# Gated linear attention and a multiplicative FFN on one core: pairs from running products instead of levels, in list-scheduled order

## Chip, core and metric

The kernel runs on one NeuronCore of one Trainium2 chip. The metric is the device time of one execution in microseconds (us), the median of several runs.

## What is computed

For each of 4 batches and 8 heads a state of 48 x 48 numbers runs over 768 tokens; every row d of it is multiplied by its own gate before the token's product is added. The result of all heads, 3072 tokens x 384, goes through the FFN.

```python
f = 1.0 / (1.0 + np.exp(-f_logit))
for t in range(S):
    state = f[:, :, t, :, None] * state + np.einsum('bhd,bhe->bhde', k[:, :, t], v[:, :, t])
    y[:, :, t] = np.einsum('bhd,bhde->bhe', q[:, :, t], state)
a = x @ w1
b = x @ w2
h = a * b @ w3
return (h @ w_out).astype(np.float32)
```

Here x is y with the heads side by side, w1 and w2 are 384 x 1024, w3 is 1024 x 1024 and w_out 1024 x 384. q, k, v and f_logit are float32; the four weights arrive as float64 and are turned to float32 on the chip.

## The kernel before, in words

The tokens are cut into 24 chunks of 128, six to a batch. The heads go in four pairs, the even head of a pair on partitions 0 to 47, the odd one on 64 to 111, so a tile of a chunk is 112 partitions x 512 columns (4 pairs x 128 tokens). Three chunks make an FFN block of 384 tokens; there are eight blocks.

- **Products of gates** (`prep_items`, lines 106 to 132): for a chunk, VectorE and ScalarE build seven levels. At level l the blocks of 2^l tokens hold q and k with the products of the gates inside the block; half of a new tile is multiplied by VectorE (line 125), the other half copied by ScalarE (line 129), once for q and once for k.
- **Attention** (`attend_items`): every pair of tokens of a chunk is taken at the level of the smallest block that holds both. `leaf` (line 171) makes products of 32 x 32 for six levels, and VectorE masks and adds them up (lines 178, 184); GpSimd copies the result into the pair matrix (line 192). `off` (lines 201, 209) adds the two coarse levels, `turn` (226) transposes k, `value` multiplies the pair matrix with v (263) and q with the state before the chunk (270), `advance` (240 to 251) renews the state, `join` (288) transposes the result into xt.
- **FFN** (`ffn_items`): for each of eight column groups, xt times w1 and xt times w2 (line 306), three products of 128 x 128 x 384 each; ScalarE copies the first (312), VectorE multiplies the second into it (315). `down` (323) multiplies with wc = w3 w_out.
- **Weights** (`weight_items`, `fetch`): 36 pieces of float64, first w_out (8), then w3 (16, two to a `fold` of eight products into wc, line 380), then w1 and w2 (12). A piece goes through VectorE (352, 353, 354), GpSimd (355), ScalarE (356, 357), VectorE (358) and GpSimd (359).

The order is written out by hand: for chunk u, the items of its attention, of the products of chunk u + 1 and a share of the waiting weights or FFN work carry a number between 0 and 1 and are emitted in that order. Each engine runs its instructions strictly in the order of emission. SP issues all DMAs.

A float32 matmul stands in the trace as two MATMUL instructions, each with its LDWEIGHTS (PEld).

## Time and profile before

| | us |
|---|---|
| median of three runs | 863.71 |
| lowest and highest run | 860.79, 870.68 |
| span of the profiled execution, the only time that its page gives | 863.2 |

| engine | busy, us | share of the span | instructions |
|---|---|---|---|
| TensorE (PE) | 701.1 | 81% | 12824 |
| VectorE (DVE) | 449.4 | 52% | 972 |
| ScalarE (ACT) | 275.7 | 32% | 757 |
| GpSimd (POOL) | 120.3 | 14% | 182 |

The span runs from the first to the last instruction of one execution. A busy share is an average over stages that differ: the stretch in which the weights are converted (to about 220 us), the long middle, and the last block. [...]

### The profile page before, as it was taken

How to read it: one execution, taken by the hardware profiler on the slowest of the kernel's cores; microseconds unless marked ns; L12 is line 12 of the kernel's file. 1: busy time of each engine (PE TensorE's matmuls, PEld its weight loads, DVE VectorE, ACT ScalarE, POOL GpSimd, SP SyncE). 2: the span in 40 equal slices, each digit the busy share in tenths (PEclk: the TensorE clock that was granted, in tenths of full speed). 3: DMA queues.
4: the chain of work that ended last, by engine and by line, in shares of the span. 5: the costliest groups of instructions: out<-in, count | busy, mean ns of one | idle time of the engine just before them, and what ended most of it. 6: DMA issues, size and time to landing. Idle time of an engine off the chain costs nothing.

```text
span 863.2 us, 28797 instructions
## 1 busy us (share of the span) xinstructions
PE 701.1 (81%) x12824; PEld 466.2 (54%) x12824; DVE 449.4 (52%) x972; ACT 275.7 (32%) x757; POOL 120.3 (14%) x182
## 2 busy tenths in 40 slices
PE   3236477642789988999999888989999998988998
PEld 2223343331456655666566556665666656665654
DVE  6866455489946255525652555355526652563010
ACT  3432222134524333233323333333334432431110
POOL 3432223154300000000000000000000000000000
PEclk9996686755899998999999889999999999998999
DMA  4421422144101021102110111011101111000000
GB/s 145 142 97 34 126 74 97 35 137 132 52 26 39 25 58 39 30 20 58 40 30 22 56 40 30 20 58 40 31 25 53 40 30 47 21 2 3 28 0 27
DMA packets 21580, 43.37 MB, mean 50 GB/s; under 512 B 3664, under 2 KB 9936, under 8 KB 21456
## 3 DMA queue, kind: packets, MB, share of 16 engines
q1 hardware_dynamic: 21456, 41.53, 15.5%
q8 instruction: 100, 1.64, 0.8%
q14 instruction: 24, 0.20, 0.1%
HBM read 36.80 MB, written 4.72 MB: 48 GB/s over the span
## 4 chain that ended last, share of the span: by engine, by line
PE 76%; issue 8%; DVE 7%; POOL 5%; ACT 2%; DMA 1%; SPq 0%; POOLq 0%; DVEq 0%; ACTq 0%
PE f L306 32%; PE f L323 15%; PE par L171 10%; PE f L380 7%; PE par L263 4%; DVE snap L125 3%; PE par L270 2%; POOL exponent L355 2%; ACT exponent L356 2%; PE par L209 2%; POOL w3s L359 1%; PE misc L240 1%; DVE exponent L358 1%; PE par L201 1%; PE misc L226 1%
## 5 line engine op out<-in xcount | busy, mean ns | idle before, releaser
L306 PE MATMUL f<-xt,w1s 128*128 128x384 f32 x384 | 150.1, 530 | 9.6 <-ACT xt L289 7.1
L306 PE MATMUL f<-xt,w2s 128*128 128x384 f32 x384 | 152.5, 537 | 2.4 <-DVE ab L315 2.4
L125 DVE TENSOR_TENSOR snap<-snap,tprod 112x256 f32<-112x256 f32 x288 | 127.6, 484 | 38.5 <-ACT snap L129 33.0
L178 DVE TENSOR_TENSOR sc<-par,mask 128x384 f32<-128x384 f32 x96 | 53.0, 552 | 164.2 <-PE par L171 164.2
L129 ACT COPY snap<-snap 112x256 f32<-112x256 f32 x312 | 110.8, 413 | 76.8 <-DVE snap L106 74.1
L323 PE MATMUL f<-wc,ab 128*128 128x384 f32 x384 | 128.2, 488 | 0.0
L171 PE MATMUL par<-snap 48*32 48x32 f32 x6144 | 84.4, 208 | 47.5 <-issue 44.4
L192 POOL COPY amt<-ad 32x256 f32<-32x256 f32 x96 | 45.9, 479 | 540.0 <-DVE ad L184 535.9
L380 PE MATMUL f<-ab,w3s 128*128 128x384 f32 x128 | 64.1, 674 | 57.5 <-POOL w3s L359 57.5
L306 PEld LDWEIGHTS f<-xt,w1s 128*128 128x128 f32 x384 | 74.0, 203 | 53.6 <-issue 11.2
L171 PEld LDWEIGHTS par<-snap 48*32 48x32 f32 x6144 | 74.3, 110 | 51.2 <-issue 47.8
L306 PEld LDWEIGHTS f<-xt,w2s 128*128 128x128 f32 x384 | 74.0, 203 | 47.4 <-issue 8.6
L323 PEld LDWEIGHTS f<-wc,ab 128*128 128x128 f32 x384 | 71.8, 190 | 47.6
L184 DVE TENSOR_REDUCE ad<-sc 128x64 f32<-128x384 f32 x96 | 78.1, 814 | 4.6
L380 PEld LDWEIGHTS f<-ab,w3s 128*128 128x128 f32 x128 | 33.6, 271 | 84.4 <-POOL w3s L359 60.1
L312 ACT COPY a<-f 128x384 f32<-128x384 f32 x64 | 30.6, 479 | 139.9 <-PE f L306 139.9
L315 DVE TENSOR_TENSOR ab<-f,a 128x384 f32<-128x384 f32 x64 | 35.4, 553 | 65.7 <-PE f L306 65.5
L356 ACT ACTIVATE exponent<-exponent 128x512 uint32<-128x512 uint32 (+1 forms) x36 | 21.8, 606 | 130.5 <-POOL exponent L355 130.5
L263 PE MATMUL par<-vt,amt 128*128 128x48 f32 x384 | 49.1, 283 | 17.1 <-ACT amt L219 16.9
L263 PEld LDWEIGHTS par<-vt,amt 128*128 128x128 f32 x384 | 49.9, 203 | 23.9 <-issue 17.5
L328 ACT COPY o<-f 128x384 f32<-128x384 f32 x24 | 11.5, 479 | 100.6 <-PE f L323 96.0
L171 PEld LDWEIGHTS par<-q,k 48*32 48x32 f32 x1536 | 22.5, 110 | 35.1 <-issue 28.7
(53 smaller groups left out, 651.7 us busy)
## 6 DMA issues: line engine op xcount, KB each, us to landing
raw<-in_w_dram SPq DMA_DIRECT2D x28, 512.0 KB, 3.5
f<-in_f_logit_dram SPq DMA_DIRECT2D x48, 96.0 KB, 2.6
q<-in_q_dram SPq DMA_DIRECT2D x48, 96.0 KB, 2.8
k<-in_k_dram SPq DMA_DIRECT2D x48, 96.0 KB, 2.2
vt<-in_v_dram SPq DMA_DIRECT2D x24, 192.0 KB, 3.0
out_dram<-o SPq DMA_DIRECT2D x24, 192.0 KB, 1.9
raw<-in_w_out_dram SPq DMA_DIRECT2D x8, 384.0 KB, 4.1
mask<-in_leaf_mask_dram SPq DMA_DIRECT2D x1, 96.0 KB, 2.3
```

What stands on the lines that cost most here:

```text
L125: nc.vector.tensor_tensor(dst[:, :, grow], src[:, :, grow], tt[:, :, 1 - grow : 2 - grow].to_broadcast([R, nb, m]), ALU.mult,)
L129: nc.scalar.copy(dst[:, :, 1 - grow], src[:, :, 1 - grow])
L171: nc.tensor.matmul(pp[par][a : a + 32, o : o + 32], lhsT=kk[rows(par), cols], rhs=qq[rows(par), cols], start=True, stop=True,)
L178: nc.vector.tensor_tensor(sc.rearrange("p h l i -> p h (l i)"), pp[par][:, 0 : 2 * NLEAF * 32].rearrange("p (h n) -> p h n", h=2), mask.re ...
L184: nc.vector.tensor_reduce(out=st["ad"][:, par, 2 * half : 2 * half + 2], in_=sc.rearrange("p h l i -> p h i l"), axis=AX.X, op=ALU.add,)
L192: nc.gpsimd.tensor_copy(amt[a : a + 32, :, :, a : a + 32], st["ad"][a : a + 32])
L263: nc.tensor.matmul(po(hp, par), lhsT=amt[:, par, hp], rhs=st["v"][:, h * D : h * D + D], start=(hp == 0), stop=first, skip_group_check=True,)
L306: nc.tensor.matmul(pu, lhsT=ws[:, kc, jc * P : jc * P + P], rhs=xts[n][:, kc], start=(kc == 0), stop=(kc == KM - 1),)
L315: nc.vector.tensor_tensor(st["ab"][jc], pu, st["a"], ALU.mult)
L323: nc.tensor.matmul(po, lhsT=st["ab"][jc][:, s * P : s * P + P], rhs=wc[:, jc], start=(jc == 0), stop=(jc == KF - 1),)
L356: nc.scalar.activation(s, s, AF.Copy, bias=-896.0 * 2.0**23, scale=2.0**23)
L380: nc.tensor.matmul(pw, lhsT=st["w"][:, kc * P : kc * P + P], rhs=wo[kc], start=(kc == 0), stop=(kc == KF - 1),)
```

## The change

- **One product per head and chunk.** For a chunk, two scans on VectorE run along the tokens: `forward` gives the product P of the gates from the chunk's second token on, `backward` the products of the gates after a token, divided by P at the chunk's end (`ends`). Q = q P and K = k times the backward product; K and Q are multiplied once per head (`pairs`, 128 x 128), VectorE masks the result with a triangle (`mask`), and the value product, now transposed, uses it as the moving operand. The lines 106 to 209 of before, their copies on ScalarE and GpSimd, and the transpose of the result are gone; ten DMAs per block from SBUF to SBUF put the result into xt. The state is kept in a block form for a pair of heads (`blocks`, on GpSimd), so the state's part of the value product is four matmuls a chunk, not eight.
- **A range test.** `judge` tests that no product at a chunk's end is below 2^-40 and that all results are finite, and writes a flag; every engine loads it after its last instruction (line 136) and, where it is set, runs `general`, the scheme of before without the conversion of weights, and without the interleaving of prep, attention and FFN.
- **Weights.** w1 and w2 come first, then w_out, then w3. The last multiplication of a piece is one VectorE instruction (line 521), which takes over the ScalarE scaling (357) and the GpSimd multiplication (359). Four buffers for raw words where there were three, 21 buffers for the products a b where there were 12, three PSUM buffers for the FFN where there were two.
- **Order.** `Plan.order` takes all work as tasks with an engine, a cost, dependences and a priority, and places at each step the task that can start first. The numbers of cost are the author's.

```diff
+NAB = 21
+FLOOR = 2.0**-60
+RANGE = 2.0**-40
...
+        while left:
+            best = None
+            for t in left:
+                if any(d["end"] is None for d in t["deps"]):
+                    continue
+                at = max(
+                    [free.get(t["eng"], 0.0)]
+                    + [d["end"] + (d["lag"] if d["eng"] != t["eng"] else 0.0) for d in t["deps"]]
+                )
+                if t["takes"]:
+                    n, taken = self.slots[t["takes"]]
+                    if len(taken) >= n:
+                        enders = freed[id(taken[-n])]
+                        if any(e["end"] is None for e in enders):
+                            continue
+                        at = max([at] + [e["end"] + e["lag"] for e in enders])
+                key = (at, t["prio"], t["no"])
+                if best is None or key < best[0]:
+                    best = (key, t)
+            (at, _, _), t = best
+            t["at"], t["end"] = at, at + t["cost"]
+            free[t["eng"]] = t["end"]
+            if t["takes"]:
+                self.slots[t["takes"]][1].append(t)
+            left.remove(t)
+            done.append(t)
+        return sorted(done, key=lambda t: (t["at"], t["no"]))
...
+        ranged(tc, q, k, f_logit, v, w1, w2, w3, w_out, out, ident, w1s, w2s, wc, left)
+        outside = nc.values_load(left[0:1, 0:1], min_val=0, max_val=1)
+        with tc.If(outside > 0, preferred_fallthrough_block=False):
+            general(tc, q, k, f_logit, v, leaf_mask, out, ident, w1s, w2s, wc)
...
+        t["lf"] = plan.add("SP", 1.2, load(fs[u % 2], f_logit), past(u, 2, "g"), n0 - 30, lag=2.2)
...
+        def gates():
+            g, f = gate[u % 2], heads(fs[u % 2])
+            nc.scalar.activation(heads(g[:, 0:NQ])[:, :, 1:C], f[:, :, 1:C], AF.Sigmoid)
+            nc.scalar.activation(lead[u % 4], f[:, :, 0], AF.Sigmoid)
+        t["g"] = plan.add("ACT", 0.85, gates, [t["lf"]] + past(u, 2, "r") + past(u, 5, "d"), n0)
...
+        def forward():
+            s["P"] = one.tile([R, NQ], F32, name="fwd")
+            nc.vector.tensor_tensor_scan(
+                s["P"], gate[u % 2][:, 0:NQ], first, 0.0, ALU.mult, ALU.add
+            )
+        t["p"] = plan.add("DVE", 1.1, forward, [t["g"]] + past(u, 1, "q", "i"), n0)
+        def ends():
+            last = heads(s["P"])[:, :, C - 1]
+            end = heads(back)[:, :, C - 1]
+            nc.vector.tensor_scalar(end, last, FLOOR, None, ALU.max)
+            nc.vector.reciprocal(end, end)
+            nc.vector.tensor_tensor(least, least, last, ALU.min)
+            if not closes:
+                s["G"] = work3.tile([R, HP], F32, name="G")
+                nc.vector.tensor_copy(s["G"], last)
...
+        def scale_q():
+            s["Q"] = work3.tile([R, NQ], F32, name="Q")
+            nc.vector.tensor_tensor(s["Q"], qs[u % 3], s["P"], ALU.mult)
...
+        def backward():
+            s["R"] = one.tile([R, NQ], F32, name="bwd")
+            nc.vector.tensor_tensor_scan(
+                s["R"][:, ::-1], gate[u % 2][:, NQ:0:-1], back[:, ::-1], 0.0, ALU.mult, ALU.add
+            )
...
+        def pairs():
+            s["pa"] = [ps.tile([P, NQ], F32, name=f"pa{par}") for par in range(2)]
+            for hp in range(HP):
+                cols = slice(hp * C, hp * C + C)
+                for par in range(2):
+                    nc.tensor.matmul(
+                        s["pa"][par][:, cols], lhsT=s["K"][rows(par), cols], rhs=s["Q"][rows(par), cols],
+                        start=True, stop=True,
+                    )
+        t["a"] = plan.add("PE", 1.2, pairs, [t["q"], t["k"]] + past(u, 1, "m0", "m1"), n0 - 1000)
...
+                    s["A"][:, par], heads(s["pa"][par]), causal.unsqueeze(1).to_broadcast([P, HP, C]), ALU.mult
...
+                s["pk"] = ps.tile([P, HP, R], F32, name="pk")
+                for hp in range(HP):
+                    nc.tensor.transpose(
+                        out=s["pk"][:, hp], in_=s["K"][:, hp * C : hp * C + C], identity=ident[0:R, 0:R]
+                    )
...
+        def value():
+            s["py"] = ps.tile([R, HP, C], F32, name="py")
+            for hp in range(HP):
+                for par in range(2):
+                    h = 2 * hp + par
+                    w = 64 if par == 0 else D
+                    nc.tensor.matmul(
+                        s["py"][64 * par : 64 * par + w, hp], lhsT=s["v"][:, h * D : h * D + w],
+                        rhs=s["A"][:, par, hp], start=(hp == 0), stop=opens, skip_group_check=True,
+                    )
+            if not opens:
+                for hp in range(HP):
+                    nc.tensor.matmul(
+                        s["py"][:, hp], lhsT=sb[(u - 1) % 2][:, hp], rhs=s["Q"][:, hp * C : hp * C + C],
+                        start=False, stop=True, skip_group_check=True,
+                    )
...
+                            s["pd"][64 * par : 64 * par + w, hp], lhsT=s["kt"][:, hp, 64 * par : 64 * par + w],
+                            rhs=s["v"][:, h * D : h * D + D], start=True, stop=True,
+                        )
...
+                nc.vector.tensor_tensor(s["G"], s["G"], lead[(u + 1) % 4], ALU.mult)
+                gain = s["G"].unsqueeze(2).to_broadcast([R, HP, D])
+                if opens:
+                    nc.vector.tensor_tensor(s["S"], s["pd"], gain, ALU.mult)
+                else:
+                    nc.vector.tensor_tensor(s["S"], s["pd"], st[u - 1]["S"], ALU.add)
+                    nc.vector.tensor_tensor(s["S"], s["S"], gain, ALU.mult)
...
+                    nc.gpsimd.tensor_copy(sb[u % 2][rows(par), :, 64 * par : 64 * par + D], s["S"][rows(par)])
...
+                blk[n]["ys"][:, :, at : at + C], s["py"], AF.Copy, accum_out=ysum[:, u : u + 1]
...
+            pa = plan.add("PE", 1.93, up(jc, 0), ready + ups[-1:], 100 * n + 50, takes="f")
...
+        def clamped():
+            nc.gpsimd.tensor_scalar(s["s"], s["s"], 896.0 + 255.0, 896.0, ALU.min, ALU.max)
+        def shifted():
+            nc.scalar.activation(s["s"], s["s"], AF.Copy, bias=-896.0 * 2.0**23, scale=2.0**23)
+        def signed():
+            nc.vector.scalar_tensor_tensor(s["s"], s["hi"], 0x80000000, s["s"], ALU.bitwise_and, ALU.bitwise_or)
+        def joined():
+            nc.vector.scalar_tensor_tensor(dst(), s["mf"], 2.0**-20, s["s"].bitcast(F32), ALU.mult, ALU.mult)
...
+        ld = plan.add("SP", 3.2 * w, load, [parts[-4]] if len(parts) >= 4 else [], prio - 20, lag=2.2)
+        e = plan.add("DVE", 0.45 * w, exponent, [ld] + parts[-3:-2], prio)
+        c = plan.add("POOL", 0.75 * w, clamped, [e], prio)
...
+    plan.add("DVE", 1.5, judge, [tk[u]["y"] for u in range(NU)], -20)
+    for t in plan.order():
+        t["emit"]()
...
-        nc.scalar.mul(mf, mf, 2.0**-20)
-        nc.vector.scalar_tensor_tensor(s, hi, 0x80000000, s, ALU.bitwise_and, ALU.bitwise_or)
-        nc.gpsimd.tensor_tensor(dst, mf, s.bitcast(F32), ALU.mult)
...
-            todo = attend_items(u)
-            if u + 1 < NU:
-                todo += [(0.05 + 0.115 * i, it) for i, it in enumerate(prep_items(u + 1))]
-            n = -(-len(queue) // (UB - u % UB))
-            todo += [((i + 0.6) / n, queue.pop(0)) for i in range(n)]
-            for _, it in sorted(todo, key=lambda x: x[0]):
-                it()
```


Two places in the order. On VectorE, in the stretch where w3 (before) and w2 (after) is converted; raw, exponent and mantissa belong to a piece of weights, snap and tprod to a level of the chunk's gate products, fwd to the new scan, ab to the FFN. Before:

```order
L352 TENSOR_SCALAR exponent<-raw 128x512
L353 TENSOR_SCALAR mantissa<-raw 128x512
L354 SCALAR_TENSOR_TENSOR mantissa<-raw,mantissa 128x512
L358 SCALAR_TENSOR_TENSOR exponent<-raw,exponent 128x512
L384 COPY wc<-f 128x384
L125 TENSOR_TENSOR snap<-snap,tprod 112x4x64 x2
L132 TENSOR_TENSOR tprod<-tprod 112x4
```


After:

```order
L501 TENSOR_SCALAR exponent<-raw 128x512
L505 TENSOR_SCALAR mantissa<-raw 128x512
L509 SCALAR_TENSOR_TENSOR mantissa<-raw,mantissa 128x512
L434 TENSOR_TENSOR ab<-f,a 128x384
L242 SCALAR_TENSOR_TENSOR fwd<-gate_99,first 112x512
L518 SCALAR_TENSOR_TENSOR exponent<-raw,exponent 128x512
L521 SCALAR_TENSOR_TENSOR w2s<-mantissa,exponent 128x512
```


A piece has five VectorE rows where it had four, and no level stands between the pieces; the FFN's product ab of block 0 and the scan of a chunk do.

On TensorE, around the first product with wc; par is the level scheme's PSUM, pa and pk the new scheme's, py the value product's. Before:

```order
L209 MATMUL par_2780<-snap 64x64
L209 MATMUL par_2781<-snap 64x64
L306 MATMUL f<-xt,w2s 128x384 x3
L323 MATMUL f<-wc,ab 128x384 x8
L263 MATMUL par_2851<-vt,amt_91 128x48
L263 MATMUL par_2852<-vt,amt_91 128x48
```


After:

```order
L285 MATMUL pa_1322<-Q,K 128x128
L285 MATMUL pa_1323<-Q,K 128x128
L308 MATMUL pk<-ident,K 128x112 x4
L454 MATMUL f<-wc,ab 128x384 x8
L326 MATMUL py<-A,vt 64x128
L326 MATMUL py<-A,vt 48x128
```


The 64 x 64 products of a level, and the 32 x 32 ones that stand ahead of them, have given way to four 128 x 128 products for each of the two halves (two rows here are one of each half) and four transposes.

## Rows read from the trace of the kernel before

**Rows 1.** Page, part 1: busy time (share of the span) and instructions, TensorE.

```profile
PE 701.1 (81%) x12824; PEld 466.2 (54%) x12824; DVE 449.4 (52%) x972; ACT 275.7 (32%) x757; POOL 120.3 (14%) x182
```

**Rows 2.** Stretches: length, then busy PE, PEld, DVE, ACT, POOL; clock, DMA share, GB/s.

```profile
0.00:220.00 220.00, 105.45 (x1769) 70.55 (x1770) 147.30 (x264) 69.12 (x159) 78.22 (x95) 0.76 0.32 102
220.00:835.00 615.00, 570.99 (x10981) 381.42 (x10981) 300.45 (x706) 204.17 (x593) 42.11 (x88) 0.94 0.11 33
632.00:710.00 78.00, 74.14 (x1570) 50.15 (x1569) 42.78 (x102) 29.34 (x86) 5.51 (x12) 0.98 0.14 41
800.00:835.00 35.00, 35.00 (x133) 21.59 (x132) 2.79 (x5) 4.88 (x12) 0.00 (x0) 1.00 0.05 18
```

**Rows 3.** Waits of TensorE: who for whom, us in total, times, longest us.

```profile
PE f L380 <- POOL w3s L359: 57.5, 8, 17.5
PE par L171 <- issue: 49.1, 25, 3.3
```

**Rows 4.** Chain that ended last, in time: start us, us, what.

```profile
144.48 8.24 PE f L380 x16
255.00 2.13 PE f L306 x6
258.83 3.89 PE f L306 x12
262.72 1.72 PE par L263 x16
282.18 5.16 PE f L323 x16
```

**Rows 5.** Timeline of TensorE, 365 to 378 us: start us, us, what.

```profile
365.84 0.68 PE L209 MATMUL par<-snap 48*64 48x64 f32 x16
366.46 0.60 PE L226 MATMUL misc<-ident,snap 112*128 112x112 f32 x4
375.82 1.10 PE L270 MATMUL par<-state,snap 48*128 48x48 f32 x16
376.84 0.67 PE L240 MATMUL misc<-vt,kt 128*64 128x48 f32 x16
```

**Rows 6.** Timeline of VectorE, then of GpSimd: start us, us, what.

```profile
6.79 0.69 DVE L106 TENSOR_TENSOR snap<-q,f 112x512 f32<-112x512 f32 x1 [6.79 <-ACT f L104]
...
184.82 0.77 DVE L354 SCALAR_TENSOR_TENSOR mantissa<-raw,mantissa 128x512 f32<-128x512 uint32 x1
189.80 0.41 DVE L352 TENSOR_SCALAR exponent<-raw 128x512 uint32<-128x512 uint32 x1
...
190.59 0.98 DVE L354 SCALAR_TENSOR_TENSOR mantissa<-raw,mantissa 128x512 f32<-128x512 uint32 x1
191.72 0.69 DVE L358 SCALAR_TENSOR_TENSOR exponent<-raw,exponent 128x512 uint32<-128x512 uint32 x1 [0.15 <-ACT exponent L356]
...
192.67 1.49 DVE L353 TENSOR_SCALAR mantissa<-raw 128x512 uint32<-128x512 uint32 x1
...
190.31 0.72 POOL L355 TENSOR_SCALAR exponent<-exponent 128x512 uint32<-128x512 uint32 x1 [0.91 <-DVE exponent L352]
192.56 1.31 POOL L359 TENSOR_TENSOR w2s<-mantissa,exponent 128x512 f32<-128x512 f32 x1 [1.54 <-DVE exponent L358]
```

**Rows 7.** Groups by line, shapes apart: busy us, mean ns of one.

```profile
L178 DVE TENSOR_TENSOR sc<-par,mask 128x384 f32<-128x384 f32 x96 | 53.0, 552 | 164.2 <-PE par L171 164.2
L184 DVE TENSOR_REDUCE ad<-sc 128x64 f32<-128x384 f32 x96 | 78.1, 814 | 4.6
L251 DVE TENSOR_TENSOR state<-state,misc 112x192 f32<-112x192 f32 x16 | 5.7, 354 | 47.5 <-PE misc L240 47.3
L132 DVE TENSOR_TENSOR tprod<-tprod 112x4 f32<-112x4 f32 x24 | 3.7, 155 | 0.0
```

**Rows 8.** Page, part 6: DMA issues, KB each, us to landing.

```profile
raw<-in_w_dram SPq DMA_DIRECT2D x28, 512.0 KB, 3.5
```

**Rows 9.** Timeline of ScalarE at the end: start us, us, what.

```profile
859.74 0.48 ACT L328 COPY o<-f 128x384 f32<-128x384 f32 x1 [4.72 <-PE f L323]
```

More of the change, by code (lines that the diff above doesn't have):

```diff
@@ L21 @@
 F32 = mybir.dt.float32
+I32 = mybir.dt.int32
 U32 = mybir.dt.uint32
@@ L39 @@
 UB = TB // C
+NB = B * S // TB
 NLEAF = 6
@@ L42, with __init__, slot, add @@
 NW = 512
+NAB = 21
+FLOOR = 2.0**-60
+RANGE = 2.0**-40
+class Plan:
+    def __init__(self):
+        self.tasks = []
+        self.slots = {}
+    def slot(self, name, n):
+        self.slots[name] = [n, []]
+    def add(self, eng, cost, emit, deps=(), prio=0.0, takes=None, frees=(), lag=0.2):
+        t = {
+            "eng": eng, "cost": cost, "emit": emit, "deps": [d for d in deps if d is not None], "prio": prio,
+            "takes": takes, "frees": list(frees), "lag": lag, "at": None, "end": None, "no": len(self.tasks),
+        }
+        self.tasks.append(t)
+        return t
+    def order(self):
+        free, done, left = {}, [], list(self.tasks)
+        freed = {}
+        for t in self.tasks:
+            for f in t["frees"]:
+                freed.setdefault(id(f), []).append(t)
+        while left:
[25 more added lines that the diff above has]
+        return sorted(done, key=lambda t: (t["at"], t["no"]))
 @with_exitstack
@@ L79 @@
     wc = const.tile([P, KF, DM], F32, name="wc")
-    amts = [const.tile([P, 2, HP, C], F32, name=f"amt{i}") for i in range(2)]
-    qkf = [[const.tile([P, NQ], F32, name=f"{nm}{i}") for nm in "qkf"] for i in range(2)]
+    left = const.tile([1, 1], I32, name="left")
+    with tc.manual_schedule():
+        ranged(tc, q, k, f_logit, v, w1, w2, w3, w_out, out, ident, w1s, w2s, wc, left)
+        outside = nc.values_load(left[0:1, 0:1], min_val=0, max_val=1)
+        with tc.If(outside > 0, preferred_fallthrough_block=False):
+            general(tc, q, k, f_logit, v, leaf_mask, out, ident, w1s, w2s, wc)
@@ new lines, in general @@
+@with_exitstack
+def general(ctx, tc, q, k, f_logit, v, leaf_mask, out, ident, w1s, w2s, wc):
+    nc = tc.nc
+    PSUM = bass.MemoryType.PSUM
+    keep = ctx.enter_context(tc.tile_pool(name="gkeep", bufs=1))
+    snap = ctx.enter_context(tc.tile_pool(name="snap", bufs=30))
+    tpool = ctx.enter_context(tc.tile_pool(name="tpool", bufs=2))
+    work = ctx.enter_context(tc.tile_pool(name="gwork", bufs=2))
+    work3 = ctx.enter_context(tc.tile_pool(name="gwork3", bufs=3))
+    abp = ctx.enter_context(tc.tile_pool(name="gabp", bufs=KF))
+    ps_par = ctx.enter_context(tc.tile_pool(name="ps_par", bufs=2, space=PSUM))
+    ps_misc = ctx.enter_context(tc.tile_pool(name="ps_misc", bufs=2, space=PSUM))
+    ps_f = ctx.enter_context(tc.tile_pool(name="gps_f", bufs=2, space=PSUM))
+    mask = keep.tile([P, NLEAF, 32], F32, name="mask")
+    amts = [keep.tile([P, 2, HP, C], F32, name=f"amt{i}") for i in range(2)]
+    qkf = [[keep.tile([P, NQ], F32, name=f"g{nm}{i}") for nm in "qkf"] for i in range(2)]
@@ L142 @@
     xts = {}
-    def rows(par):
-        return slice(64 * par, 64 * par + D)
     def pair():
@@ L403 @@
[L403 to L428 removed]
+    for tiles in qkf:
+        for t in tiles:
+            nc.gpsimd.memset(t[32:64], 0.0)
@@ L432 @@
+    load(0)
+    nc.sync.dma_start(mask, leaf_mask)
+    load(1)
+    for amt in amts:
+        nc.gpsimd.memset(amt, 0.0)
+    for u in range(NU):
+        for item in prep_items(u):
+            item()
+        for _, item in attend_items(u):
+            item()
+        if u % UB == UB - 1:
+            for item in ffn_items(u // UB):
+                item()
 _OUTS = [((B * S, DM), "float32")]
```

379 lines of the change are left out of this document (299 added, 80 removed).

## Prediction

> **What bounds the kernel now.** I read the page's busy times first: TensorE is busy 701.1 us of 863.2, and no other engine comes near it [rows 1]. An average hides stages, so the busy time by stretch is next [rows 2]. To 220 us TensorE is busy less than half of the time (105 us) at a mean granted clock of 0.76, while VectorE is busy 147 us: there the conversion of the weights runs ahead of everything. From 220 to 835 us TensorE is busy 93% at 0.94 and nothing else matters. The waits say what it lacks: 57.5 us for a piece of w3 from GpSimd (all in the front), and 49.1 us in which the products of 32 x 32 waited for nothing but their own instruction stream [rows 3]. So there are two separate limits, the weights' chain in front and the amount of TensorE work behind it, and the change touches both. The chain in order of time then gives what each piece of TensorE work costs on the path [rows 4].
>
> **TensorE's work after the change.** The FFN is as before. Two column groups (12 instructions) take 3.89 us, so one product of xt with w1 or w2 takes 1.945; a product with wc takes 5.16, and a fold is the same shape (it took 8.24 in the front, partly at the lower clock) [rows 4]. 128 x 1.945 + 24 x 5.16 + 8 x 5.16 = 249.0 + 123.8 + 41.3 = 414.1 us. TensorE's other 287 us (701.1 - 414.1) are the level scheme and the lower clock.
>
> Attention, per chunk. The transposes stay at 0.60 and the state update at 0.67 [rows 5]. The state's part of the value product has eight instructions of 128 columns; 384 columns take 324 ns (3.89 / 12), so 128 take 108: 0.86 us. `pairs`, 16 instructions, does not occur before. Its nearest row from below is the state's product, also 48 partitions in alternating halves with 128 weight columns: 1.10 us for 16; from above full-height products that load 128 columns each, 1.72 [rows 4, 5]. I take 1.4. The chunk's own value product has 16 instructions with 64 or 48 weight columns and 128 moving ones: 1.72 if one follows the other, 0.86 if the two column halves run side by side. The products of 48 x 64 took 0.68 for 16, 42 ns each, where 64 columns one after the other would be 54 [rows 5], so some overlap exists; I take 1.25. That is 24 x 2.65 + 20 x 2.13 (no update behind a batch's last chunk, no state in its first) = 63.6 + 42.6 = 106.2, between 89.6 and 125.2. TensorE's work is then 414.1 + 106.2 = 520.3 us, in some 5,200 matmul instructions instead of 12,824, and the 32 x 32 stream that starved is gone.
>
> **The front.** TensorE can't work freely before wc exists, since only 21 products a b can be kept, and wc needs all of w_out and w3. So I sum VectorE's rows up to the last `joined` of w3, which the order gives, and ask what TensorE can have done by then.
>
> - VectorE's first work starts near 7 us, as now [rows 6].
> - A weight piece of 512 columns: exponent 0.41, the mantissa, an instruction of the same kind, as much, the rounding 0.98, the sign 0.69 [rows 6]. The rounding took 0.77 once with GpSimd quiet and 0.98 beside the clamp [rows 6]; the clamp stays beside it, so I take 0.98. The new `joined` is of the sign's kind: between 0.69 and 0.98, I take 0.75, near the contiguous one. Sum 3.24; 28 of these are 90.7. The eight pieces of 384 columns at 2.5 (about three quarters) are 20. Together 110.7.
> - Seven chunks of attention stand before it. The scan occurs nowhere. From below it is a plain product of its size, 0.69 [rows 6]; from above twice the rate that the reduction shows, 2.2. The reduction itself, the only row in which a result waits on the one before, takes 814 ns for 384 elements [rows 7], 1.09 for 512: I take 1.1. 15 scans 16.5; 14 products by 0.69 are 9.7; 14 masks of 512 columns at 0.552 x 4/3 = 0.74 are 10.3; nine state instructions at 0.35 and 32 four-column ones at 0.155 [rows 7] are 8.2. Together 44.7.
> - Ten products a b and seven copies to wc, at the mask's 0.55 [rows 7]: 9.4.
> - VectorE's own waits. It runs in order, so a mask waits for `pairs` with the weights queued behind it, and TensorE is at the lower clock in the first chunks. I allow 8; at worst see the rivals.
>
> 7 + 110.7 + 44.7 + 9.4 + 8 = 179.8 us. Raw words don't hold it up: 512 KB land in 3.5 us [rows 8], four are in flight and a piece takes 3.24. What goes from the front is GpSimd's multiplication of 1.31 per piece; beside it a mantissa took 1.49, where the like exponent took 0.41 [rows 6].
>
> The last fold follows: 5.16 to 8.24, I take 6.7, which makes 186.5. By then TensorE has done eight folds (41.3), 21 products with w1 or w2 (40.8), seven `pairs` and value products (18.6), six transposes and updates (7.6) and five state parts (4.3): 112.6 us. 520.3 - 112.6 = 407.7 remain, and there is always FFN work for the gaps of attention, so they follow without a break: 594.2.
>
> **What comes on top.** Where the FFN follows other work, its first product took 2.13 instead of 1.945 [rows 4]; of 30 such places in the order I count 24 here, 4.5 us. The clock: 0.98 in a stretch with attention, 1.00 in one of pure FFN [rows 2]; 1% of 408 is 4. The end: the last copy starts at 859.74 and the span ends at 863.2 [rows 9], so 3.5 stay. Each engine then loads a flag and branches past 5,000 instructions; no row shows a branch, so the bounds are nothing and one wait for the instruction stream, 3.3 at most [rows 3]; I take 2. 594.2 + 4.5 + 4 + 3.5 + 2 = 608.2. The sum is made against the profiled execution's span of 863.2, half a microsecond below the median of the runs, 863.7; so I forecast 609.
>
> Edits costed at nothing: the SBUF-to-SBUF gathers for xt, some 4 us of issue and a landing of a few us per block, lie beside the FFN of the block before; only block 0's is open, and VectorE's weights cover it. GpSimd's copies into the block state lie beside TensorE's FFN. `judge` comes behind the last chunk with more than 200 us of FFN left. If the cover of the gathers went, eight times about 6 us would come on top.
>
> [...]
>
> [...]
>
> **Rivals.**
> - *The front isn't filled.* Today VectorE is busy only 67% of the front [rows 2], since it waits in order for others. At 80% the 172 us of its work would take 215, 35 more than I take: 644. For it: masks wait behind `pairs`, which stand behind products with w1 in TensorE's order, at half clock. Against: the detour through GpSimd's multiplication and the levels are gone, and there is always a further piece to convert. 0.13.
> - *Slow scans.* At 2.2 the 15 scans of the front cost 16.5 more, and with as much waiting behind them 12: 637. Behind the front they can't bind: 17 chunks at about 9 us of VectorE are 153 of 408. 0.10.
> - *The clock doesn't stay up.* At 0.94 as today [rows 2] 408 us become 433: 634. For it: attention still comes in short pieces. Against: 0.98 over 78 us that hold such pieces. 0.12.
> - *Attention cheap, VectorE fast.* All lower bounds: attention behind the front 12 less, joins and roundings 8, scans 6, no waits 8: 575. With most of it 585. 0.15.
> - *The range test fails.* One lane of one chunk below 2^-40, or one result that isn't finite, is the point from which it decides: then the levels and the FFN run again behind everything. Today 615 us hold 21 of 24 chunks interleaved [rows 2], so at least 609 + 615 = 1224, slower than before. Against: over the inputs that the reference draws the smallest such product is 2^-30.2. With it I count that the list order stalls in some way I don't see so badly that nothing is won. 0.04.
> - The forecast, 595 to 625: 0.46.
>
> Without the two ends, the range runs from 580 to 652. Faster by over 1% is every case but the range test's: 0.95, within 1% 0.01, slower 0.04; 1% is about what runs that spread from 860.8 to 870.7 can tell.
>
> **What would show it.** Right: the last join of w3 near 180 us with VectorE busy over 90% to there; from 190 us TensorE busy over 97% at a clock of 0.97 or more; `pairs` at 1.1 to 1.7 us for 16, scans near 1.1 us; no instruction of `general`; 3 to 7 us between TensorE's last matmul and the end. Wrong: TensorE idle behind 200 us, waits of VectorE in front for more than 30 us, scans over 1.6, or a clock below 0.95 behind the front.

## The result, and the profile after

The changed kernel takes 590.60 us (median of four runs, 589.80 to 591.19) where the kernel before takes 865.98 (four runs, 860.79 to 870.68): a ratio of 0.681, interval 0.677 to 0.685. The forecast was 609 with a range from 580 to 652. The profiled execution has a span of 588.6 us, 274.6 less than before. I split that by TensorE, first from part 1 of the page, which answers to [rows 1]:

```profile
PE 530.0 (90%) x2610; PEld 332.3 (56%) x2610; DVE 281.4 (48%) x558; ACT 108.1 (18%) x241; POOL 58.0 (10%) x94
```

TensorE is busy 171.1 us less (701.1 to 530.0), with a fifth of the matmul instructions, and idle 103.5 us less (863.2 - 701.1 = 162.1 before, 588.6 - 530.0 = 58.6 now). Nearly half of the second part are the waits that [rows 3] put down to issue, 49.1 us, in which the 32 x 32 products waited for nothing that the profile shows (that their instruction stream starved is the prediction's reading, no row shows it): no such wait stands among TensorE's waits below. Where the rest of the idle time lies, the stretches show (columns as in [rows 2]; the clock is TensorE's granted one, 0.50 from 180 to 220 us in the kernel before, 1.00 the highest in any stretch):

```profile
0.00:60.00 60.00, 31.16 (x188) 22.42 (x189) 48.29 (x92) 13.57 (x27) 17.80 (x32) 0.77 0.53 161
60.00:120.00 60.00, 48.78 (x234) 29.84 (x233) 57.52 (x118) 16.77 (x35) 14.43 (x22) 0.89 0.52 158
120.00:180.00 60.00, 54.17 (x248) 33.02 (x247) 57.10 (x107) 13.60 (x29) 9.08 (x12) 0.97 0.54 158
0.00:176.00 176.00, 130.10 (x640) 82.46 (x642) 158.94 (x306) 43.27 (x90) 41.30 (x66) 0.87 0.54 160
176.00:580.00 404.00, 399.60 (x1972) 249.83 (x1972) 122.46 (x254) 64.36 (x152) 16.70 (x28) 1.00 0.15 45
```

The first 60 us are half empty; to 176 us TensorE lacks 46 us in all, and from 176 to 580 only 4.4. What it waits for (columns as in [rows 3]):

```profile
PE pa L285 <- DVE K L276: 18.8, 4, 10.4
PE f L572 <- DVE w3s L521: 10.5, 2, 10.0
PE f L419 <- DMA xt<-ys: 7.1, 5, 4.0
PE py L326 <- ACT ys L378: 4.4, 3, 1.6
```

The 57.5 us for pieces of w3 have become 10.5. More than half of the first wait is the start of the program, 10.4 us until the first K; the third is mostly block 0's gathers of xt. The last, three waits until ScalarE has emptied the value product's PSUM buffer (1.24, 1.63 and 1.53 in the timeline, at 265, 325 and 382 us), is the 4.4 us behind 176.

The pieces of attention in TensorE's timeline (start, us, what; these answer to [rows 5]) and the last fold of w3:

```profile
163.50 1.16 PE L285 MATMUL pa<-Q,K 48*128 48x128 f32 x16
164.59 0.60 PE L308 MATMUL pk<-ident,K 112*128 112x112 f32 x4
...
170.58 5.32 PE L572 MATMUL f<-wo,w3s 128*128 128x384 f32 x16
...
182.63 1.09 PE L326 MATMUL py<-A,vt 128*64 128x128 f32 x16
183.65 1.13 PE L332 MATMUL py<-Q,sb 112*112 112x128 f32 x8
184.71 0.67 PE L348 MATMUL pd<-vt,kt 128*64 128x48 f32 x16
```

A piece's cost on the path is the distance to the next start: `pairs` 1.09, the transposes 0.44, the chunk's value product 1.02 (182.63 to 183.65), the state's part 1.06, the update 0.59: 4.20 us a chunk.

VectorE at the last piece of w3 (answers to [rows 6]):

```profile
161.19 0.42 DVE L501 TENSOR_SCALAR exponent<-raw 128x512 uint32<-128x512 uint32 x1
161.52 0.42 DVE L505 TENSOR_SCALAR mantissa<-raw 128x512 uint32<-128x512 uint32 x1
161.98 0.98 DVE L509 SCALAR_TENSOR_TENSOR mantissa<-raw,mantissa 128x512 f32<-128x512 uint32 x1
162.88 1.21 DVE L242 TENSOR_TENSOR_SCAN fwd<-gate,first 112x512 f32<-112x512 f32 x1
164.01 0.53 DVE L579 COPY wc<-f 128x384 f32<-128x384 f32 x1
...
167.65 0.68 DVE L521 SCALAR_TENSOR_TENSOR w3s<-mantissa,exponent 128x512 f32<-128x512 f32 x1
```

The scan's row shows 1.21 us, and the next instruction starts 1.13 behind it (162.88 to 164.01); the exponent's shows 0.42, with the next start after 0.33. The last `joined` of w3 starts at 167.65. The end, from ScalarE's last copy and from the branches on the flag (second view, TensorE's sequencer and SP: count, least, median and greatest ns, first and last start):

```profile
580.38 0.48 ACT L463 COPY o<-f 128x384 f32<-128x384 f32 x1 [4.68 <-PE f L454]
```

```profile
L137 PEldq COMPARE_BRANCH  x2: 95/1744/3393, 575.0 to 580.5; - x2
...
L137 SPq COMPARE_BRANCH  x2: 38/46/53, 582.2 to 584.3; - x2
```

SP's first instruction behind the branch (the same columns):

```profile
L948 SPq EVENT_SEMAPHORE  x10: 17/28/28, 587.3 to 588.6; - x10
```

8.2 us lie between the start of the last copy and the end of the span (588.6 - 580.38), where [rows 9] have 3.5; 4.3 of them lie behind SP's last branch. For 3.0 of these 4.3 SP shows no instruction (584.3 to 587.3). ScalarE and VectorE stand as long between their last branch and their next instruction (3.1 and 2.9 us in the trace), GpSimd only 0.4; TensorE's branch at 580.5 takes 3.39 itself.

### The profile page after: what moved, and what is told of

It reads as the page before. It is cut to its first block, busy times and chain, and to the rows that moved or that the text cites. A ratio compares the mean times of both kernels' runs of the same rounds, so it can differ in the third digit from the quotient of the medians.

```text
span 588.6 us, 6990 instructions
## 1 busy us (share of the span) xinstructions
PE 530.0 (90%) x2610; PEld 332.3 (56%) x2610; DVE 281.4 (48%) x558; ACT 108.1 (18%) x241; POOL 58.0 (10%) x94
## 4 chain that ended last, share of the span: by engine, by line
PE 78%; DVE 10%; SPq 4%; DMA 2%; issue 1%; ACT 1%; POOL 0%; ACTq 0%; POOLq 0%
PE f L419 41%; PE f L454 18%; PE pa L285 5%; SPq L400 4%; PE py L326 4%; PE py L332 4%; PE f L572 3%; DMA xt<-ys 2%; PE pk L308 2%; DVE exponent L518 2%; PE pd L348 2%; DVE mantissa L509 2%; DVE bwd L268 1%; DVE mantissa L505 1%; DVE w3s L521 1%
## 5 line engine op out<-in xcount | busy, mean ns | idle before, releaser
L419 PEld LDWEIGHTS f<-xt,w2s 128*128 128x128 f32 x384 | 73.0, 192 | 49.4 <-issue 1.5
L572 PE MATMUL f<-wo,w3s 128*128 128x384 f32 x128 | 46.0, 517 | 10.5 <-DVE w3s L521 10.5
L285 PE MATMUL pa<-Q,K 48*128 48x128 f32 x384 | 30.6, 304 | 18.8 <-DVE K L276 18.8
L369 POOL COPY sb<-S 48x192 f32<-48x192 f32 x40 | 27.7, 691 | 178.8 <-PE py L332 80.5
L296 DVE TENSOR_TENSOR A<-pa,causal 128x512 f32<-128x512 f32 x48 | 30.7, 678 | 25.1 <-PE py L326 18.0
L572 PEld LDWEIGHTS f<-wo,w3s 128*128 128x128 f32 x128 | 25.8, 204 | 29.3 <-DVE w3s L521 11.7
L326 PE MATMUL py<-A,vt 128*64 128x128 f32 (+1 forms) x384 | 30.9, 298 | 11.4 <-ACT ys L378 4.4
L285 PEld LDWEIGHTS pa<-Q,K 48*128 48x128 f32 x384 | 25.8, 204 | 25.7 <-DVE K L276 10.9
L242 DVE TENSOR_TENSOR_SCAN fwd<-gate,first 112x512 f32<-112x512 f32 x24 | 29.4, 1225 | 2.9 <-ACT gate L233 2.8
L509 DVE SCALAR_TENSOR_TENSOR mantissa<-raw,mantissa 128x512 f32<-128x512 uint32 (+1 forms) x36 | 29.5, 820 | 0.9
L268 DVE TENSOR_TENSOR_SCAN bwd<-gate,back 112x512 f32<-112x512 f32 x24 | 29.7, 1237 | 0.0
```

The lines of the kernel that those rows point to most:

```text
L242: nc.vector.tensor_tensor_scan(s["P"], gate[u % 2][:, 0:NQ], first, 0.0, ALU.mult, ALU.add)
L268: nc.vector.tensor_tensor_scan(s["R"][:, ::-1], gate[u % 2][:, NQ:0:-1], back[:, ::-1], 0.0, ALU.mult, ALU.add)
L285: nc.tensor.matmul(s["pa"][par][:, cols], lhsT=s["K"][rows(par), cols], rhs=s["Q"][rows(par), cols], start=True, stop=True,)
L296: nc.vector.tensor_tensor(s["A"][:, par], heads(s["pa"][par]), causal.unsqueeze(1).to_broadcast([P, HP, C]), ALU.mult)
L326: nc.tensor.matmul(s["py"][64 * par : 64 * par + w, hp], lhsT=s["v"][:, h * D : h * D + w], rhs=s["A"][:, par, hp], start=(hp == 0), stop= ...
L369: nc.gpsimd.tensor_copy(sb[u % 2][rows(par), :, 64 * par : 64 * par + D], s["S"][rows(par)])
```

## Experiments

My theory: two limits in sequence. In front, the sum of VectorE's work up to the last join of w3 sets when TensorE can work freely; behind it TensorE's own work is the bound. The rival: the front is set by something else, the order or TensorE's lack of other work, so that VectorE's sum is not the price. Twelve kernels follow, most of them the changed kernel with one edit.

**The changed kernel again**, beside the first experiments.

> The changed kernel itself, for a comparison on one chip. Every theory: 588 to 592 us, span near 588.6.

590.51 us (590.16 to 591.06). Differences below are taken from this. The kernel before took 863.24 us beside this one and the next three, 862.87 beside the kernels with SP's costs or the priorities changed (these ran on another chip), and 867.34 beside the rest.

**No flag, no branch.**

```diff
-        outside = nc.values_load(left[0:1, 0:1], min_val=0, max_val=1)
-        with tc.If(outside > 0, preferred_fallthrough_block=False):
-            general(tc, q, k, f_logit, v, leaf_mask, out, ident, w1s, w2s, wc)
```

> The range test is still computed, but no engine loads the flag and there is no branch and no general scheme (so the guard is left out). My theory: the end grew from 3.4 us before (859.74 to 863.2) to 8.2 us (580.38 to 588.6) because SP loads the flag, waits for its queues and jumps only after the last copy; without it 4 to 5 us less, some 585.5 us of time and an end of 3 to 4 us. Rival: the end is the last transfer and the close of the program, and the flag lies beside them: within 1 us of the changed kernel.

586.87 us (585.70 to 587.57), 3.6 less. ScalarE's timeline at the end:

```profile
582.13 0.48 ACT L460 COPY o<-f 128x384 f32<-128x384 f32 x1 [4.68 <-PE f L451]
```

With a span of 585.6 the last copy starts 3.5 us before the end, as in [rows 9]. So 4.7 of the 8.2 us (8.2 - 3.5) belong to loading the flag and branching; the medians differ by less, as TensorE ends 1.75 us later here (582.13 - 580.38). 3.0 of the 4.7 are the stretch behind SP's last branch in which SP shows no instruction (584.3 to 587.3); what it stands for there no row shows. If the rest of the end is as long as without the branch, the other 1.7 lie ahead of that branch, where SP's load of the flag takes 0.52 us (line 136, at 581.3) and eight semaphore instructions of line 137 stand from 582.3 to 584.2.

**The products of `pairs` twice.**

```diff
-            for hp in range(HP):
+            for hp in [h for h in range(HP) for _ in range(2)]:
```

> Each product of K and Q is issued twice. My theory: behind the last fold (176 us) TensorE is the bound without a gap, so 17 chunks cost 17 x 1.09 = 18.5 us in full, and the seven before it, at the lower clock or beside waits, 0 to 8: 607 to 617 us. Rival: VectorE, in order, sets the pace of the chunks until attention ends, and TensorE's extra work falls into its waits: under 597 us.

610.81 us (610.11 to 612.20), 20.3 more. The page's part 1:

```profile
PE 550.3 (90%) x2994; PEld 353.9 (58%) x2994; DVE 282.2 (46%) x558; ACT 108.0 (18%) x241; POOL 58.1 (10%) x94
```

TensorE is busy 20.3 us more (530.0 to 550.3) and idle 58.1 instead of 58.6: the 384 further instructions, 53 ns each, fill no idle time and come on top. From the end of the last fold to TensorE's last product it takes 419.6 us instead of 404.4, so 15.2 more for 17 chunks, 0.89 a chunk where I had taken 1.09; the other 4.7 lie in front. The second half of the theory stands.

**Lighter conversion**: no mantissa and no rounding instruction, 40 us off VectorE.

```diff
-            nc.vector.scalar_tensor_tensor(dst(), s["mf"], 2.0**-20, s["s"].bitcast(F32), ALU.mult, ALU.mult)
+            nc.vector.scalar_tensor_tensor(dst(), s["hi"].bitcast(F32), 2.0**-20, s["s"].bitcast(F32), ALU.mult, ALU.mult)
...
-        m = plan.add("DVE", 0.45 * w, mantissa, [ld, e], prio)
-        r = plan.add("DVE", 0.7 * w, rounded, [m], prio)
-        g = plan.add("DVE", 0.7 * w, signed, [h, r], prio)
+        g = plan.add("DVE", 0.7 * w, signed, [h], prio)
```

> A weight piece without its mantissa and rounding instructions (two of five on VectorE; the weights come out wrong, everything else is computed as before). My theory: VectorE sets the front. It loses 36 x about 1.1 = 40 us, the last join of w3 comes near 130 us instead of 168, and TensorE's idle time ahead of it, some 45 us with the lower clock, shrinks to about 15: 555 to 568 us. Rival: the front is set by TensorE's own order and clock and by xt: 582 us or more, with VectorE waiting instead.

586.84 us (584.34 to 588.00): 3.7 less, far outside what I expected. VectorE's work did go, but not the time to 176 us (one stretch, columns as above):

```profile
0.00:176.00 176.00, 138.75 (x666) 89.42 (x667) 123.48 (x243) 42.24 (x90) 42.15 (x66) 0.86 0.52 161
```

VectorE is busy 35 us less there (158.94 to 123.48), yet the last fold starts at 164.95, only 5.6 us earlier than the 170.58 above. VectorE's timeline shows it standing still:

```profile
33.95 0.76 DVE L501 TENSOR_SCALAR exponent<-raw 128x512 uint32<-128x512 uint32 x2
39.11 0.69 DVE L518 SCALAR_TENSOR_TENSOR exponent<-raw,exponent 128x512 uint32<-128x512 uint32 x1 [4.40 <-ACT exponent L515]
...
43.58 0.69 DVE L518 SCALAR_TENSOR_TENSOR exponent<-raw,exponent 128x512 uint32<-128x512 uint32 x1 [1.39 <-ACT exponent L515]
```

Between two conversions it waits 4.40 and 1.39 us for ScalarE, and the order has put no scan or product of the next chunk into these gaps. The first half of my theory, that VectorE's sum alone sets the front, falls. The order is the suspect: `Plan.order` books SP for 3.2 us per piece of weights. By its own numbers SP is taken 28 x 3.2 + 8 x 2.4 for weights and 7 x 4.8 for the q, k, v and f_logit of seven chunks, 142 us. SP's timeline in the changed kernel says otherwise:

```profile
45.54 6.31 SPq L400 DMA_DIRECT2D xt<-ys  x10
...
53.01 0.93 SPq L218 DMA_DIRECT2D f<-in_f_logit_dram  x2
54.04 0.37 SPq L495 DMA_DIRECT2D raw<-in_w_dram  x1
...
58.79 0.35 SPq L227 DMA_DIRECT2D vt<-in_v_dram  x1
```

A piece of weights takes SP 0.37 us, the two issues of f_logit 0.93, v 0.35, and the ten gathers of xt, booked at 1.5, take 6.31. The prediction's some 4 us for these ten were an estimate, near ten times the 0.42 us that one issue of v takes in the kernel before.

**SP's costs as the trace shows them**, in three kernels: with the lighter conversion, alone, and with priorities that put the chunks ahead of w3; then these priorities alone. The first two:

```diff
-        t["lf"] = plan.add("SP", 1.2, load(fs[u % 2], f_logit), past(u, 2, "g"), n0 - 30, lag=2.2)
+        t["lf"] = plan.add("SP", 0.9, load(fs[u % 2], f_logit), past(u, 2, "g"), n0 - 30, lag=2.2)
...
-        t["lv"] = plan.add("SP", 1.2, load_v, past(u, 4, "v", "s"), n0 - 27, lag=2.2)
+        t["lv"] = plan.add("SP", 0.4, load_v, past(u, 4, "v", "s"), n0 - 27, lag=2.2)
...
-            "SP", 1.5, emit, [tk[u]["y"] for u in range(n * UB, n * UB + UB)] + ([blk[n - 2]["up"]] if n >= 2 else []),
+            "SP", 6.0, emit, [tk[u]["y"] for u in range(n * UB, n * UB + UB)] + ([blk[n - 2]["up"]] if n >= 2 else []),
...
-        ld = plan.add("SP", 3.2 * w, load, [parts[-4]] if len(parts) >= 4 else [], prio - 20, lag=2.2)
+        ld = plan.add("SP", 0.4, load, [parts[-4]] if len(parts) >= 4 else [], prio - 20, lag=2.2)
```

> The light weights again (mantissa and rounding left out, the weights come out wrong), with other costs of SP in the list: 0.4 for a raw load instead of 3.2, 0.9 and 0.4 for the chunk loads instead of 1.2, 6.0 for a gather instead of 1.5, as the trace shows SP to take. New theory A: with less VectorE work the front was held by the order, in which SP is thought busy 3.2 us per raw load, so that conversions are put late; the last join of w3 moves from 162 to some 130 to 140 us and the time from 586.8 to 556 to 572. Theory B: the front is then TensorE's own chain at the lower clock, whatever the list thinks of SP: 582 us or more.

569.11 us (568.81 to 569.93). TensorE's last fold (timeline):

```profile
138.12 5.34 PE L570 MATMUL f<-wo,w3s 128*128 128x384 f32 x16
```

It starts 26.8 us earlier than with the old costs (164.95). With SP's costs mended, the removal of the same VectorE work is worth 16 us (against the next kernel), where it was worth 3.7.

> The changed kernel with the same other costs of SP and nothing else. Theory A: with full weights VectorE is the bound of the front (busy 157 of its first 168 us), but the list still holds loads apart; a gain of 5 to 18 us, 572 to 586. Theory B, or VectorE's sum alone: no gain, 587 to 594.

585.06 us (583.91 to 585.33), 5.5 less. This rests on two chips, and the two kernels' intervals against the kernel before (0.675 to 0.680 and 0.681 to 0.689) all but meet; either way the costs alone change little. With the full conversion VectorE is nearly filled already: it is busy 161.9 of the first 176 us, 158.9 in the changed kernel. The third kernel has the same costs and

```diff
-        return 9.0 * u if u < UB else 45.0 + 17.0 * (u - UB)
+        return 9.0 * u if u < UB else 35.0 + 12.0 * (u - UB)
...
-            at[0] += 2.6
+            at[0] += 4.0
```

> SP's costs as before this, and the priorities changed so that the chunks of the second and third block come ahead of w3 (a weight piece every 4.0 instead of 2.6, a chunk from the fourth on at 35 + 12 per chunk instead of 45 + 17). Theory C: what TensorE lacks in the front is FFN work, 21 products with w1 and w2 of 41 us where the 21 buffers would let it do 42 of 81; with two more blocks' xt there it does them while w3 is converted, though the last join comes later, near 200 us: 555 to 572 us. Against it: wc later means everything later, as with the sum by which I predicted (last join plus the rest): 600 us or more.

567.02 us (566.08 to 568.22), a ratio to the kernel before of 0.656 (0.654 to 0.659): 23.5 us, 4%, less than the changed kernel, and the best version I have. Stretches, and the last fold:

```profile
60.00:120.00 60.00, 55.53 (x339) 35.52 (x339) 56.98 (x118) 17.93 (x41) 10.06 (x18) 1.00 0.51 155
120.00:180.00 60.00, 60.00 (x357) 38.36 (x356) 57.06 (x111) 15.58 (x34) 16.24 (x19) 1.00 0.48 151
```

```profile
209.47 5.32 PE L572 MATMUL f<-wo,w3s 128*128 128x384 f32 x16
```

The last fold starts at 209.47, 39 us *later* than in the changed kernel, and the kernel is still faster: from 60 to 180 us TensorE is busy 115.5 us instead of 103.0. Its idle time falls from 58.6 to 43.5 (566.5 - 523.0, the page's busy time), and TensorE is busy 7 us less with the same 2610 instructions, at a granted clock of 1.00 from 60 to 120 us where the changed kernel has 0.89. So the last join doesn't set the end, nor does VectorE's sum up to it; what TensorE finds to do in front counts for more. VectorE's work isn't free by this: with SP's costs mended, 40 us less of it brought 16. What the lighter conversion would bring with these priorities wasn't run. Of the 43.5 us that TensorE is still idle, 30.1 lie in the first 60 us.

> The changed priorities with SP's costs as they were. Theory C alone: most of the gain of the run before, 565 to 582 us. If the gain of that run is SP's costs: 587 us or more.

The two priorities without SP's costs: 574.40 us (573.57 to 575.07), 16.1 less. The priorities bring most of the gain, SP's costs the last 7.4.

**w3 first**: w1 and w2 are fetched behind w3, as before the change; their loop moves to the end of `weights`.

```diff
-        for half in range(2):
-            cols = slice(half * NW, half * NW + NW)
-            for which, (d, w) in enumerate(((w1s, w1), (w2s, w2))):
...
+        for half in range(2):
+            cols = slice(half * NW, half * NW + NW)
+            for which, (d, w) in enumerate(((w1s, w1), (w2s, w2))):
```

> The weights in the order of the kernel before, w_out, w3, then w1 and w2, still list-scheduled. My theory: the order of the weights is a part of the gain, since w1 and w2 first let TensorE do 21 products of the FFN (41 us) while VectorE still converts; with w3 first they come behind the front: 612 to 630 us. Rival: VectorE's front is as long in any order and TensorE makes good with attention: 588 to 598 us.

608.11 us (607.98 to 608.24), 17.6 more: 3.9 below the range of my theory, and 10 above the rival's. One stretch:

```profile
120.00:180.00 60.00, 42.16 (x236) 28.49 (x238) 51.25 (x97) 14.68 (x34) 9.83 (x13) 0.79 0.49 147
```

The last fold starts at 109.63, long before wc is needed, and TensorE, without w1 and w2, is busy 42 of 60 us here, where the changed kernel has 54.

**Order by hand**: the changed kernel's tasks, sorted by a share of a chunk as in the kernel before, in place of the earliest start.

```diff
-                key = (at, t["prio"], t["no"])
+                key = (t["hand"], at, t["no"])
...
+    for u in range(NU):
+        mine = chunk_tasks[u]
+        for i, x in enumerate(mine):
+            x["hand"] = u + i / len(mine)
+        n = -(-len(queue) // (UB - u % UB))
+        for i in range(n):
+            queue.pop(0)["hand"] = u + (i + 0.6) / n
+        if u % UB == UB - 1:
+            queue += ffn_tasks[u // UB]
```

> The new tasks and the new weights' order, but emitted in the manner of the kernel before: the tasks of a chunk in the order they are written, the waiting weights or FFN tasks spread evenly among them, no costs. My theory: TensorE's work is the same 520 us, but each chunk's chain from scan to value product stands undivided on the in-order engines and TensorE waits for VectorE at every chunk: 620 to 670 us. Rival: the order is worth little, because TensorE has FFN work between any two steps: under 605 us.

738.64 us (737.75 to 739.53), 148 more; I had the direction, but expected 30 to 80. TensorE's waits (line numbers two higher):

```profile
PE pa L287 <- DVE K L278: 83.0, 16, 30.8
PE f L421 <- DMA xt<-ys: 46.4, 22, 5.2
PE f L574 <- DVE w3s L523: 28.3, 11, 5.3
```

`pairs` now waits for K 16 times, 83.0 us, where the list order leaves 4 such waits: by hand, the scans, K and `pairs` of one chunk stand in one row of items, and what fills TensorE meanwhile is only what a share of the queue puts there; the gathers of xt, free in the forecast, cost 46.4. The share of the gain that the list order holds isn't 148 by this, since a better order by hand may exist; it is what this one costs. Even so it takes 128.7 us less than the kernel before beside it (867.34): the new tasks and the weights' order keep nearly half of the gain without the list.

**The range test fails**, so the general scheme runs too.

```diff
-RANGE = 2.0**-40
+RANGE = 2.0**-20
```

> The bound of the range test is raised from 2^-40 to 2^-20, which the inputs don't meet, so the level scheme runs behind the new one. My theory (the rival of the prediction on the other side): the branch is taken on every engine and attention by levels and the FFN run again, 590 + 615 at least, 1200 to 1400 us. Rival: most of the second pass overlaps the first one's end or is cheaper than in the kernel before, since no weights are converted: under 1150 us.

1591.69 us (one run), beyond both ranges. Stretches before and behind the flag:

```profile
0.00:590.00 590.00, 531.79 (x2658) 334.06 (x2658) 283.73 (x563) 109.81 (x246) 62.68 (x102) 0.96 0.26 81
590.00:1590.00 1000.00, 747.13 (x12648) 536.46 (x12648) 338.46 (x816) 248.83 (x679) 37.82 (x96) 0.69 0.08 24
```

The general scheme adds 1001 us, more than the whole kernel before takes (863.7), though it converts no weights: TensorE is busy 75% at a granted clock of 0.69, where [rows 2] have 93% at 0.94. I had priced it at the rate of the kernel before, where attention and FFN are interleaved; that this is the whole difference isn't shown.

**The join alone, in the kernel before**: VectorE's `joined` for the scaling on ScalarE and the multiplication on GpSimd, and nothing else.

```diff
-        nc.scalar.mul(mf, mf, 2.0**-20)
...
-        nc.gpsimd.tensor_tensor(dst, mf, s.bitcast(F32), ALU.mult)
+        nc.vector.scalar_tensor_tensor(dst, mf, 2.0**-20, s.bitcast(F32), ALU.mult, ALU.mult)
```

> The kernel before, with only the last step of the conversion changed as in the new one: one VectorE instruction in place of a ScalarE scaling and a GpSimd multiplication. My theory: GpSimd's multiplication of 1.3 us slowed VectorE beside it (a level pair of 1.82 us where 0.76 is usual), so the front gets shorter by 36 x 0.3 to 0.5, 10 to 20 us: 845 to 856 us. Rival: VectorE was the front's bound and gets 36 x 0.69 = 25 us of extra work: 866 us or more.

850.61 us (846.41 to 854.82) beside 867.34, ratio 0.981, interval 0.958 to 1.003: as expected by its median, but no change lies inside the interval. TensorE's waits:

```profile
PE f L379 <- DVE w3s L358: 49.4, 8, 15.3
PE par L171 <- issue: 48.0, 25, 2.8
```

The wait for w3 is 49.4 where [rows 3] have 57.5. What this part is worth by itself stays open, from nothing to 4%.

## Why the prediction was right, point by point

The sum gave 608.2 for the span, 588.6 came: right in sign, in mechanism (a front, then TensorE's work without a break) and within the range, 20 us high. By its steps:

- **The front, 179.8 forecast, last join at 168.4.** The terms were right: 110.7 + 44.7 + 9.4 = 164.8, and the same rows of the trace, in the same counts, have durations of 109.2, 46.1 and 9.4; with 2.1 for setting up, VectorE's 288 rows to the last join add up to 166.8. The step that was off is adding them up: neighbours overlap (in the rows above by 0.09, 0.42 shown and 0.33 from start to start, and by 0.08 behind the scan), so VectorE is busy only 151.6 us of 168.4, 15.2 less, 0.05 per row. VectorE's idle time is 16.8, for the 15 allowed for start and waits. 179.8 + 2.0 - 15.2 + 1.8 = 168.4. The scan, which no row of before showed, has 1.23 us on average, 1.13 from start to start where a row follows at once, for 1.1 taken.
- **The last fold** ends at 175.8 for 186.5, 10.7 less: 11.4 from the front, and 0.7 back, since 7.4 us lie between the last join and its end (a product with w1 stands before it) for 6.7 taken. By then TensorE had done just what I counted: 21 products with w1 or w2, eight folds, seven `pairs` and value products, six transposes and updates, five state parts.
- **TensorE's rest, 416.2 with changeovers and clock (407.7 + 4.5 + 4), measured 404.5 (175.8 to 580.3).** Attention was oversized: 4.20 us a chunk for 4.78. `pairs` came out at its lower bound (1.09 for 1.4), the transposes by the distance to the next start and not by their row (0.44 for 0.60), the update likewise (0.59 for 0.67), the value product 1.02 for 1.25, and only the state's part cost more (1.06 for 0.86). Over the 17 `pairs` and value products, 14 transposes and updates and 15 state parts that were left, this is 10.0 us. A changeover costs 0.10 (2.04 from 165.03 to 167.07, where 1.94 is a product) for 0.19, 2.1 us; the clock of 1.00 saves the 4. The 4.4 us of waits for the value product's buffer were not in the sum. -10.0 - 2.1 - 4 + 4.4 = -11.7.
- **The end, 5.5 forecast, 8.3 measured (580.3 to 588.6)**, outside the 3 to 7 that I gave as a sign: the branch was taken at 2 with an upper bound of 3.3; by the kernel without it, it costs 4.7. The bound was the longest of the waits that [rows 3] put down to issue; the gap behind SP's branch alone is 3.0, and SP's load of the flag (0.52) and the semaphores of line 137 come before it.
- -10.7 - 11.7 + 2.8 = -19.6, and 608.2 - 19.6 = 588.6.

Two counts were misread without touching the sum: the 5,200 matmul instructions are 2610 of the kind of which the kernel before has 12,824 (with the LDWEIGHTS they would be 5,220), and the twelve instructions of 3.89 us are one column group with both its products, not two.

The rivals: the slow scans, the clock that stays down and the failing test didn't occur; "attention cheap, VectorE fast" came in part, with 590 between its 585 and my 609. "The front isn't filled" was stated wrongly: VectorE is filled, TensorE isn't. The reason of mine that the runs overturned is that I gave the front's price as VectorE's sum. The lighter conversion shows that this sum isn't what the time hangs on as long as the order believes SP to be full, and the kernel whose last join comes 39 us later and which ends 22 us earlier shows that the last join isn't either. The forecast held because the changed kernel does carry out that sequence; as advice on what to do next it would have led to the wrong edit.

What a clamp on GpSimd costs the rounding and the sign beside it, rows of VectorE and GpSimd show:

```profile
41.51 0.98 DVE L509 SCALAR_TENSOR_TENSOR mantissa<-raw,mantissa 128x512 f32<-128x512 uint32 x1
...
43.09 1.09 DVE L518 SCALAR_TENSOR_TENSOR exponent<-raw,exponent 128x512 uint32<-128x512 uint32 x1
...
44.82 0.69 DVE L509 SCALAR_TENSOR_TENSOR mantissa<-raw,mantissa 128x512 f32<-128x512 uint32 x1
```

```profile
41.23 0.72 POOL L512 TENSOR_SCALAR exponent<-exponent 128x512 uint32<-128x512 uint32 x1 [4.68 <-DVE exponent L501]
42.91 0.72 POOL L512 TENSOR_SCALAR exponent<-exponent 128x512 uint32<-128x512 uint32 x1 [0.96 <-DVE exponent L501]
```

The rounding takes 0.98 beside a clamp and 0.69 alone, the sign 1.09 beside the next clamp. The rounding starts 0.28 behind its clamp's start, the sign 0.18, and both end 0.54 or 0.55 us behind their clamp's end (41.95 and 43.63). So do all 24 roundings and signs of 512 columns in front that start with more than 0.14 us of a clamp left. What is lost is thus what is left of the clamp at the start, less 0.14. The 24 lose 7.4 us together, where my sum, by 0.98 for 0.77 in 36 roundings, held 8. The 0.77 of [rows 6], which the prediction reads as a rounding with GpSimd quiet, isn't one: from 182.77 on GpSimd's copies of line 192 stand beside it in the kernel before.

```profile
182.77 3.07 POOL L192 COPY amt<-ad 32x256 f32<-32x256 f32 x4 [1.25 <-DVE ad L184]
```

## What to carry over

Before an engine's summed work is called the bound, take some of it away and look whether the end moves: here 40 us of VectorE's work in front bought 3.7, and 16 only after the order's false cost for SP was mended. Where a program orders the work by costs, hold every cost against the trace, the cheap queues first: an issue that takes 0.37 us was booked at 3.2. In a stage that starves the bound engine, ask which order gives it other work (here chunks ahead of w3, 23.5 us with the mended costs) before asking how its supplier gets faster, and add up starts, not durations.

## What the hardware showed that I had not expected

- A flag loaded by every engine and a branch that isn't followed by the other scheme still cost 4.7 us at the end of the program, 3.6 in the medians; TensorE's last branch takes 3.4 us, and between their last branch and their next instruction VectorE, SP and ScalarE stand 2.9, 3.0 and 3.1 us, GpSimd 0.4.
- A rounding or sign of 512 columns on VectorE that starts in front with more than 0.14 us of a clamp on GpSimd left ends 0.54 to 0.55 us behind the clamp, whenever it started (24 of 24): its row of 0.69 becomes 0.84 to 1.10.
- The granted clock of a short stretch and the durations in it need not agree. In the changed kernel's first and second profile `pairs` of the third chunk takes 2.08 us in both, against 1.16 in the row at 163.50 above; the stretch around it (30 to 35 us) is granted 0.50 in the first, 1.00 in the second. First profile, timeline and stretch:

```profile
32.05 2.08 PE L285 MATMUL pa<-Q,K 48*128 48x128 f32 x16 [6.75 <-DVE K L276]
```

```profile
30.00:35.00 5.00, 2.95 (x20) 2.47 (x20) 4.90 (x9) 0.63 (x1) 1.45 (x2) 0.50 0.42 143
```

Second profile:

```profile
32.23 2.08 PE L285 MATMUL pa<-Q,K 48*128 48x128 f32 x16 [6.25 <-DVE K L276]
```

```profile
30.00:35.00 5.00, 2.77 (x20) 2.47 (x20) 4.90 (x9) 0.63 (x1) 1.45 (x2) 1.00 0.39 141
```

Before each TensorE had been idle for over 6 us; the second chunk's `pairs`, at 17.52 in the first profile, takes 2.08 too, after 0.68 of idle time and in a stretch granted 1.00 (15 to 20 us). What makes these rows longer isn't shown. In front I therefore go by durations and not by the granted clock; from 176 us on that is 1.00, and the rows of `pairs` at 185.30 and 194.78 take 1.16.
